# Centring the first two row tiles before their transposes, and applying 1/std when V leaves PSUM

## The chip, the cores and the metric

The kernel runs on one core of a Trainium2 chip. A core has a matrix engine (TensorE, PE in the profile), a vector engine (VectorE, DVE), an activation engine (ScalarE, ACT), a general engine (GpSimd, POOL) and a queue engine that issues most DMAs (SyncE, SP). Each of them works through its own instructions in order and waits on semaphores for the others. The metric is the device time of one execution in microseconds; less is better.

## The reference

One transformer layer on 2048 rows of 1024 in bf16: pre-norm attention with 32 heads of width 32 and a causal window of 256, then a feed-forward part of width 3584, each with a residual. The norm has no weights.

```python
def _layernorm(x, axis=-1, eps=1e-5):
    m = jnp.mean(x, axis=axis, keepdims=True)
    v = jnp.var(x, axis=axis, keepdims=True)
    return (x - m) / jnp.sqrt(v + eps)

x = A_x
h = x + _A_ref(_layernorm(x, axis=-1), A_wqkv, A_wo)
h2 = h + _B_ref(_layernorm(h, axis=-1), B_w1, B_w2)
```

Here `_A_ref` computes `qkv = x @ wqkv`, the windowed softmax attention and the product with `wo`; `_B_ref` is `silu(x @ w1) @ w2`. What matters for the change is that `(x - m) / std` times a weight matrix is the same as `(x - m)` times that matrix with each row divided by its std afterwards.

## The kernel before

The 2048 rows are four blocks of 512, each of four row tiles of 128. For a block, the rows are normalised (`ln_stats`, `ln_root`, `ln_norm`), transposed into `lnT_b` (features on the partitions), and multiplied with the weights: `v_group(b, j, c)` makes 512 columns of V for one row tile, `qk_group` makes 128 columns of Q or K for a whole block. Each group is eight matmuls of 128x512 into one PSUM bank (`next_acc` goes round the banks in `acc_banks`), and one copy takes the bank to SBUF. Later blocks, the attention and the feed-forward part are woven together so that TensorE always has matmuls.

The order on each engine is the order in which the Python code calls it; a manual schedule is set, so nothing is reordered. DMAs go out in order on the queue that issues them, SP for nearly all.

The change lies in the head, which makes block 0's V while the first rows and weights still arrive. Its steps before:

- SP issues row tile 0, the first half of the V weights (columns 0 to 511 of V, 1 MB, `load_wqkv(2 * D)`), row tile 2, the second half, row tile 3 and the first 512 Q columns. ACT's queue issues row tile 1 (L135, L139).
- A memset on VectorE (L157) feeds eleven matmuls on zeros (L162), which keep TensorE busy until there is data.
- For row tile 0: statistics on VectorE (L166, L174), the square root on ACT (L201), the reciprocal on VectorE (L208), and the normalisation in four quarters, three on VectorE (L194) and one on ACT (L217). Each quarter is turned by two TensorE transposes (L223), and ACT copies the result from PSUM to `lnT_b` (L224, `turn_first`).
- Row tile 1 the same with all quarters on VectorE. Row tile 2 is normalised in one instruction and turned by TensorE later. Row tile 3 is normalised in one instruction and turned by one DMA transpose that SP issues (L198, `ln_transpose`).
- Behind that transpose SP issues the remaining three loads of Q and K weights (L139), then the four row tiles of block 1 (L135).
- TensorE's order: transposes of tile 0; V of tile 0, columns 0 to 511, with the transposes of tile 1 among its matmuls and those of the next group; V of tile 1, columns 0 to 511; V of tiles 0 and 1, columns 512 to 1023, with tile 2's transposes between; V of tiles 2 and 3; then Q and K (L245, L255). ACT copies V out of PSUM (L247), two banks in turn.
- While Q and K of block 0 run, their banks are emptied by ACT and VectorE in turn (L257), and VectorE does the statistics of block 1 between its own copies.

Of the kernel before, what the change touches and what calls it, by code (L numbers as in the profile page):

```python
# [9 lines left out]
F32 = mybir.dt.float32  # L10
I32 = mybir.dt.int32
ACT = mybir.ActivationFunctionType
ALU = mybir.AluOpType

P = 128
# [29 lines left out]
def kernel(  # L45
# [10 lines left out]
    nc = tc.nc  # L56
# [3 lines left out]
    S, D = x2d.shape  # L60
# [4 lines left out]
    KT = D // P  # L65
# [4 lines left out]
    scale = float(DH) ** -0.5  # L70

    const = ctx.enter_context(tc.tile_pool(name="const", bufs=1))
    small = ctx.enter_context(tc.tile_pool(name="small", bufs=2))
# [12 lines left out]
    r_e = big.tile([P, 13312], BF16, name="r_e")  # L86
# [4 lines left out]
    tp_ps = [tp_pool.tile([P, 1024], BF16, name=f"tp{i}") for i in range(4)]  # L91
    o_ps = [ps.tile([P, 8, 64], F32, name=f"o_ps{i}") for i in range(2)]
    acc_ps = [ps.tile([P, 512], F32, name=f"acc{i}") for i in range(2)]

    def view(region, off, *dims):
        n = 1
        for d in dims:
            n *= d
        ap = region[:, off:off + n]
        if len(dims) == 2:  # L100
            return ap.rearrange("p (a b) -> p a b", b=dims[1])
        if len(dims) == 3:
            return ap.rearrange("p (a b c) -> p a b c", b=dims[1], c=dims[2])
        return ap
# [4 lines left out]
    lnT_b = [view(r_w, 24576, KT, 512), view(r_t, 0, KT, 512)]  # L109
    x_ring = [view(r_o, i * 1024, 1024) for i in range(8)]  # L110
# [17 lines left out]
    wqkv_v = A_wqkv.rearrange("(kt p) n -> p kt n", p=P)  # L128
# [5 lines left out]
    def load_x(b, j, queue=nc.sync):  # L134
        queue.dma_start(out=x_ring[(b % 2) * 4 + j], in_=x2d[(b * 4 + j) * P:(b * 4 + j + 1) * P, :])  # L135

    def load_wqkv(c0):
        dst = wqk[:, :, c0:c0 + 512] if c0 < 2 * D else wv[:, :, c0 - 2 * D:c0 - 2 * D + 512]
        nc.sync.dma_start(out=dst, in_=wqkv_v[:, :, c0:c0 + 512])  # L139

    eps = const.tile([P, 1], F32, name="eps")
    nc.vector.memset(eps[:], LN_EPS)
# [1 line left out]
    nc.scalar.activation(out=dummy[:], in_=eps[:], func=ACT.Sqrt)  # L144

    load_x(0, 0)
    load_wqkv(2 * D)
    load_x(0, 1, nc.scalar)
    load_x(0, 2)
    load_wqkv(2 * D + 512)  # L150
    load_x(0, 3)
    load_wqkv(0)

    ident = const.tile([P, P], BF16, name="ident")
    make_identity(nc, ident[:])
    warm = view(r_e, 0, 2, 512)
    nc.vector.memset(warm, 0.0)  # L157
    nc.gpsimd.memset(v[:, :, :, DH:VW], 1.0)


    for i in range(11):
        nc.tensor.matmul(o_ps[i % 2][:].rearrange("p a b -> p (a b)"), lhsT=warm[:, 0, 0:P], rhs=warm[:, 0, :], start=True, stop=True)  # L162


    def ln_half(xt, stats, c):
        nc.vector.bn_stats(out=stats[:, c, :], in_=xt[:, c * 512:(c + 1) * 512])  # L166

    def ln_stats(xt, st, j, half_done=None):
        stats = half_done
        if stats is None:  # L170
            stats = small.tile([P, 2, 6], F32, name="ln_st", tag="ln_st")
            ln_half(xt, stats, 0)
        ln_half(xt, stats, 1)
        nc.vector.bn_aggr(out=st[:, j, :], in_=stats[:])  # L174
# [18 lines left out]
    def ln_norm(xt, st, rs, j):  # L193
        nc.vector.tensor_scalar(out=xt, in0=xt, scalar1=st[:, j, 0:1], scalar2=rs[:, j:j + 1],  # L194
                                op0=ALU.subtract, op1=ALU.mult)

    def ln_transpose(xt, dst, j):
        nc.sync.dma_start_transpose(out=dst[:, :, j * P:(j + 1) * P], in_=xt)  # L198

    def ln_root(st, rs, j):  # L200
        nc.scalar.activation(out=rs[:, j:j + 1], in_=st[:, j, 1:2], func=ACT.Sqrt, bias=eps[:], scale=1.0)  # L201

    def ln_first(xt, st, rs, j, parts, on_act=0):

        if on_act:
            shift = small.tile([P, 2], F32, name="ln_shift", tag="ln_shift")
            nc.scalar.activation(out=shift[:, 0:1], in_=st[:, j, 0:1], func=ACT.Identity, scale=-1.0)
        nc.vector.reciprocal(out=rs[:, j:j + 1], in_=rs[:, j:j + 1])  # L208
        if on_act:
            nc.scalar.activation(out=shift[:, 1:2], in_=shift[:, 0:1], func=ACT.Identity, scale=rs[:, j:j + 1])  # L210
        n = 1024 // parts
        for h in range(parts):
            part = xt[:, h * n:(h + 1) * n]
            if h < parts - on_act:
                ln_norm(part, st, rs, j)
            else:
                nc.scalar.activation(out=part, in_=part, func=ACT.Identity, bias=shift[:, 1:2], scale=rs[:, j:j + 1])  # L217

    def turn_first(j, h):

        for i in range(2):
            kt = h * 2 + i
            nc.tensor.transpose(out=tp_ps[h][:, i * P:(i + 1) * P], in_=x_ring[j][:, kt * P:(kt + 1) * P], identity=ident[:])  # L223
        nc.scalar.copy(out=lnT_b[0][:, h * 2:(h + 1) * 2, j * P:(j + 1) * P],  # L224
                       in_=tp_ps[h][:, 0:256].rearrange("p (k q) -> p k q", q=P))

# [7 lines left out]
    acc_banks = list(a[:] for a in acc_ps)  # L234
# [5 lines left out]
    def v_group(b, j, c, copy, between=None):  # L240
        acc = next_acc()
        for kt in range(KT):
            if between:
                between(kt)
            nc.tensor.matmul(acc, lhsT=lnT_b[b % 2][:, kt, j * P:(j + 1) * P], rhs=wv[:, kt, c * 512:(c + 1) * 512],  # L245
                             start=(kt == 0), stop=(kt == KT - 1))
        copy(out=v[:, b * 4 + j, c * 16:(c + 1) * 16, 0:DH], in_=acc.rearrange("p (h d) -> p h d", d=DH))  # L247
# [204 lines left out]
    dve, act = nc.vector.tensor_copy, nc.scalar.copy  # L452


    st, rs = ln_tiles("a")
    half = small.tile([P, 2, 6], F32, name="ln_st", tag="ln_st")
    ln_stats(x_ring[0], st, 0)
    ln_root(st, rs, 0)
    ln_half(x_ring[1], half, 0)
    ln_first(x_ring[0], st, rs, 0, 4, 1)  # L460
    ln_stats(x_ring[1], st, 1, half)
    for h in range(4):
        turn_first(0, h)
        if h == 2:
            ln_root(st, rs, 1)
    ln_first(x_ring[1], st, rs, 1, 4)
    ln_stats(x_ring[2], st, 2)

    held = []

    def turn_1(kt):
        if kt == 7:
            turn_first(1, 0)

    def turn_1_rest(kt):
        if kt == 2:
            turn_first(1, 3)
            act(**held.pop())
            ln_root(st, rs, 2)

    v_group(0, 0, 0, lambda **args: held.append(args), turn_1)
    turn_first(1, 1)
    turn_first(1, 2)
    v_group(0, 1, 0, act, turn_1_rest)
    ln_first(x_ring[2], st, rs, 2, 1)
    ln_stats(x_ring[3], st, 3)
    ln_root(st, rs, 3)
    ln_first(x_ring[3], st, rs, 3, 1)
    ln_transpose(x_ring[3], lnT_b[0], 3)
    for c0 in (D, 512, D + 512):  # L490
        load_wqkv(c0)
    v_group(0, 0, 1, act)
    for h in range(4):
        turn_first(2, h)
    v_group(0, 1, 1, act)
    v_group(0, 2, 0, act)
    v_group(0, 2, 1, act)
    nc.scalar.activation(out=dummy[:], in_=eps[:], func=ACT.Exp)
    v_group(0, 3, 0, act)
    v_group(0, 3, 1, act)  # L500

    ps_tp.__exit__(None, None, None)
    ps_sc = tc.tile_pool(name="ps_sc", bufs=1, space=bass.MemoryType.PSUM, reuse_waits="tile")
# [214 lines left out]
```

The softmax here doesn't subtract the row's maximum and nothing guards it: scores larger than these inputs give would overflow.

## Time and profile before

| | |
|---|---|
| median of 9 runs | 692.93 us (692.89 to 693.18) |
| the profiled execution | 692.96 us |
| its span, first to last instruction | 691.0 us |
| TensorE busy | 676.7 us, 98% of the span |
| VectorE, ACT, POOL busy | 290.6, 241.9, 161.0 us |
| first matmul on data (V) | 7.51 us after the span's start |
| first matmul of Q and K | 22.41 us |
| granted TensorE clock | 1.00 throughout |

Times in the profile are counted from the span's start. A row of the timeline gives start, duration, engine, line, operation, the tile written and the tiles read, the shapes, a count where like instructions were merged, and in brackets how long the engine was idle before and what released it. `SPq` and `ACTq` are instructions that issue DMAs; their duration is that of the issue, and the time until the data is there is given for a line as "DMA to landing".

### The profile page before, as it was taken

How to read it: one execution, taken by the hardware profiler on the slowest of the kernel's cores; microseconds unless marked ns; L12 is line 12 of the kernel's file. 1: busy time of each engine (PE TensorE's matmuls, PEld its weight loads, DVE VectorE, ACT ScalarE, POOL GpSimd, SP SyncE). 2: the span in 40 equal slices, each digit the busy share in tenths (PEclk: the TensorE clock that was granted, in tenths of full speed). 3: DMA queues.
4: the chain of work that ended last, by engine and by line, in shares of the span. 5: the costliest groups of instructions: out<-in, count | busy, mean ns of one | idle time of the engine just before them, and what ended most of it. 6: DMA issues, size and time to landing. Idle time of an engine off the chain costs nothing.

```text
span 691.0 us, 14107 instructions
## 1 busy us (share of the span) xinstructions
PE 676.7 (98%) x5895; PEld 331.6 (48%) x6011; DVE 290.6 (42%) x609; ACT 241.9 (35%) x463; POOL 161.0 (23%) x295
## 2 busy tenths in 40 slices
PE   8999999999999999999999999999999999999998
PEld 3444555555555555544444444444444444444445
DVE  5267646744444449533316133343133251333111
ACT  5326666666676666421310033300133100233000
POOL 1007666666666656500000000000000000000000
PEclk9999999999999999999999999999999999999999
DMA  7732241136241989971023410022300024100010
GB/s 255 246 59 74 40 89 51 26 63 184 72 131 17 243 235 288 212 270 52 11 83 110 91 39 0 1 91 69 85 0 1 25 88 94 39 1 1 30 39 24
DMA packets 76463, 60.95 MB, mean 88 GB/s; under 512 B 50288, under 2 KB 60528, under 8 KB 76400
## 3 DMA queue, kind: packets, MB, share of 16 engines
q1 hardware_dynamic: 76256, 59.78, 31.7%
q8 instruction: 47, 0.77, 0.4%
q10 hardware_dynamic: 144, 0.26, 0.1%
q14 instruction: 16, 0.13, 0.1%
HBM read 39.85 MB, written 8.39 MB: 70 GB/s over the span
## 4 chain that ended last, share of the span: by engine, by line
PE 97%; issue 1%; DMA 1%; SPq 0%; DVE 0%
PE hacc L628 19%; PE hacc L665 17%; PE acc L255 16%; PE acc L665 10%; PE acc L628 9%; PE acc L245 8%; PE acc L276 7%; PE o_ps L388 5%; PE sc L308 3%; PE hacc L276 1%; DMA r_w<-in_A_wqkv_dram 1%; PE sc L360 1%; PE sc L334 1%; PE tp L223 0%; SPq L135 0%
## 5 line engine op out<-in xcount | busy, mean ns | idle before, releaser
L378 POOL TENSOR_SCALAR_AFFINE_SELECT r_e<-r_e 128x512 bf16<-128x512 bf16 (+1 forms) x288 | 158.0, 564 | 125.6 <-ACT r_e L368 62.1
L665 PEld LDWEIGHTS <-r_a 128*128 128x128 bf16 x952 | 90.9, 98 | 103.0
L628 PEld LDWEIGHTS <-r_w 128*128 128x128 bf16 x896 | 87.4, 98 | 105.0
L665 PE MATMUL hacc<-r_a 128*128 128x512 bf16 (+2 forms) x607 | 121.8, 359 | 0.5
L628 PE MATMUL hacc<-r_e,r_w 128*128 128x512 bf16 x444 | 99.7, 379 | 0.5
L320 ACT ACTIVATE r_e<-sc 128x768 bf16<-128x768 f32 x96 | 78.2, 814 | 48.3 <-PE sc L308 48.3
L637 ACT ACTIVATE r_n<-hacc 128x512 f32<-128x512 f32 x30 | 17.9, 597 | 178.9 <-PE hacc L628 175.5
L665 PE MATMUL acc<-r_a 128*128 128x512 bf16 x329 | 73.5, 379 | 0.4
L255 PEld LDWEIGHTS <-r_w 128*128 128x128 bf16 x512 | 44.2, 97 | 46.2 <-issue 1.0
L255 PE MATMUL acc<-r_t,r_w 128*128 128x512 bf16 x233 | 60.3, 379 | 2.4 <-issue 1.7
L257 DVE CAST r_a<-acc 128x512 bf16<-128x512 f32 x56 | 38.6, 690 | 56.5 <-PE acc L255 43.6
L255 PE MATMUL acc<-r_w 128*128 128x512 bf16 x240 | 58.0, 379 | 1.5 <-issue 1.0
L388 PEld LDWEIGHTS <-r_e 128*128 128x128 bf16 x1440 | 47.4, 96 | 17.9
L276 PE MATMUL acc<-r_o,r_a 128*128 128x512 bf16 x188 | 49.5, 379 | 1.9 <-issue 1.3
L628 PE MATMUL acc<-r_e,r_w 128*128 128x512 bf16 x213 | 48.9, 379 | 0.3
L388 PE MATMUL o_ps<-r_a,r_e 128*128 128x33 bf16 x1440 | 48.1, 178 | 0.1
L680 DVE SCALAR_TENSOR_TENSOR r_t<-hacc,r_t 128x512 bf16<-128x512 f32 (+2 forms) x22 | 14.0, 635 | 56.6 <-PE hacc L665 55.2
L321 ACT ACTIVATE r_e<-sc 128x256 bf16<-128x256 f32 x96 | 37.4, 390 | 0.0
L680 DVE SCALAR_TENSOR_TENSOR r_t<-acc,r_t 128x512 bf16<-128x512 f32 x12 | 8.3, 692 | 64.2 <-PE acc L665 58.8
L638 DVE SCALAR_TENSOR_TENSOR r_a<-r_n,hacc 128x512 bf16<-128x512 f32 x30 | 20.7, 688 | 33.0 <-ACT r_n L637 33.0
L628 PE MATMUL hacc<-r_a,r_w 128*128 128x512 bf16 x139 | 32.6, 379 | 0.3
L276 PEld LDWEIGHTS <-r_a 128*128 128x128 bf16 x256 | 21.8, 97 | 22.3
(79 smaller groups left out, 532.0 us busy)
## 6 DMA issues: line engine op xcount, KB each, us to landing
r_w<-in_B_w_dram SPq DMA_DIRECT2D x8, 896.0 KB, 5.0
r_a<-in_B_w_dram SPq DMA_DIRECT2D x7, 1024.0 KB, 7.3
r_w<-in_A_wqkv_dram SPq DMA_DIRECT2D x6, 1024.0 KB, 9.0
h_dram<-r_t SPq DMA_DIRECT2D x16, 256.0 KB, 2.7
r_t<-h_dram SPq DMA_DIRECT2D x16, 256.0 KB, 2.9
out_dram<-r_t SPq DMA_DIRECT2D x31, 128.0 KB, 1.7
r_o<-in_A_x_dram SPq DMA_DIRECT2D x15, 256.0 KB, 4.0
r_e<-h_dram SPq DMA_DIRECT2D x3, 1024.0 KB, 5.6
```

The costliest lines, as they stand in the source:

```text
L245: nc.tensor.matmul(acc, lhsT=lnT_b[b % 2][:, kt, j * P:(j + 1) * P], rhs=wv[:, kt, c * 512:(c + 1) * 512], start=(kt == 0), stop=(kt == KT ...
L255: nc.tensor.matmul(acc, lhsT=wqk[:, kt, col0:col0 + P], rhs=lnT_b[b % 2][:, kt, :], start=(kt == 0), stop=(kt == KT - 1))
L257: copy(out=(qT, kT)[which][b][:, g, :], in_=acc)
L276: nc.tensor.matmul(acc, lhsT=qT[b][:, g, j * P:(j + 1) * P], rhs=wo[:, g, c * 512:(c + 1) * 512], start=(g == 0), stop=(g == G - 1))
L308: nc.tensor.matmul(sc[hh // 2][half * 64:half * 64 + 64, hh % 2, col:col + qb - qa], lhsT=kT[t // 4][r0:r0 + DH, g, k0:k0 + 64], rhs=qT[b] ...
L320: nc.scalar.activation(out=tri[:, :, :, 64:256], in_=both, func=ACT.Exp, scale=scale)
L321: nc.scalar.activation(out=e[:, 1024:1280].rearrange("p (h q) -> p h q", q=P), in_=bank[:, :, 192:320], func=ACT.Exp, scale=scale)
L378: nc.gpsimd.affine_select(out=dst, in_=src, pattern=[[0, n] for n in dst.shape[1:-1]] + [[sgn, P]], compare_op=ALU.is_ge if upper else ALU ...
L388: nc.tensor.matmul(o_ps[pair][:, qt * 2 + hh, 0:VW], lhsT=chunk_of(i, bank, piece, pair, hh), rhs=v[:, b * 4 + kt, g * 4 + pair * 2 + hh, ...
L628: nc.tensor.matmul(acc, lhsT=w1[:, kt, ft * P:(ft + 1) * P], rhs=ln2T[b][:, kt, :], start=(kt == 0), stop=(kt == KT - 1))
L665: nc.tensor.matmul(acc[:, 0:c1 - c0], lhsT=gT[:, ft, j * P:(j + 1) * P], rhs=w2[ft // 4][:, ft % 4, c0:c1], start=(ft == 0), stop=(ft == F ...
L680: nc.vector.scalar_tensor_tensor(out=t_out[j % 2][:, c0:c1], in0=acc[:, 0:c1 - c0], scalar=0.5, in1=t_in[j % 2][:, c0:c1], op0=ALU.mult, o ...
```

## The change

Row tiles 0 and 1 are no longer normalised before they are turned. Their means are found first (for tile 0 half by ACT with a summed activation and half by VectorE's statistics, for tile 1 by ACT alone), VectorE writes centred copies into `x_mid` in quarters, and these are turned and used for V. The four V groups of tiles 0 and 1 are held in four PSUM banks (the two of `o_ps` are added for the time), and ACT empties them with 1/std as the scale of each row. The statistics, roots and reciprocals are placed by when these evacuations and tile 2 need them; tile 2's copies from PSUM come ahead of the last held evacuation. Q and K need fully normalised rows, so tiles 0 and 1 are also normalised in place later, and turned by two more DMA transposes, issued behind tile 3's and ahead of the three weight loads.

Around it: row tile 1 is loaded on SP's queue, second; the halves of the V weights come in four and two pieces; the warm-up's memset covers 128 columns and its matmuls, nine in place of eleven, read them with a repeated pattern.

```diff
-    def load_wqkv(c0):
+    def load_wqkv(c0, parts=1):
         dst = wqk[:, :, c0:c0 + 512] if c0 < 2 * D else wv[:, :, c0 - 2 * D:c0 - 2 * D + 512]
-        nc.sync.dma_start(out=dst, in_=wqkv_v[:, :, c0:c0 + 512])
+        n = KT // parts
+        for k in range(0, KT, n):
+            nc.sync.dma_start(out=dst[:, k:k + n, :], in_=wqkv_v[:, k:k + n, c0:c0 + 512])
+
+    warm = view(r_e, 0, P)
+    nc.vector.memset(warm, 0.0)
...
     load_x(0, 0)
-    load_wqkv(2 * D)
-    load_x(0, 1, nc.scalar)
+    load_x(0, 1)
+    load_wqkv(2 * D, 4)
     load_x(0, 2)
-    load_wqkv(2 * D + 512)
+    load_wqkv(2 * D + 512, 2)
     load_x(0, 3)
     load_wqkv(0)
...
-    for i in range(11):
-        nc.tensor.matmul(o_ps[i % 2][:].rearrange("p a b -> p (a b)"), lhsT=warm[:, 0, 0:P], rhs=warm[:, 0, :], start=True, stop=True)
+    wide = bass.AP(tensor=warm.tensor, offset=warm.offset, ap=[warm.ap[0], [0, 4], warm.ap[1]])
+    for i in range(9):
+        nc.tensor.matmul(o_ps[i % 2][:].rearrange("p (a c) b -> p a (c b)", c=2), lhsT=warm, rhs=wide, start=True, stop=True)
...
+    x_mid = [view(r_e, 1024 + 1024 * j, 1024) for j in range(2)]
+    scrap = view(r_e, 3072, 1024)
+    mean = small.tile([P, 3], F32, name="mean")
+    half = small.tile([P, 2, 6], F32, name="ln_half")
+
+    def mean_first():
+
+        nc.scalar.activation(out=scrap[:, 0:512], in_=x_ring[0][:, 512:1024], func=ACT.Identity, scale=-1.0 / D, accum_out=mean[:, 0:1])
+        ln_half(x_ring[0], half, 0)
+        nc.vector.tensor_scalar(out=mean[:, 1:2], in0=half[:, 0, 1:2], scalar1=half[:, 0, 4:5], scalar2=-0.25, op0=ALU.add, op1=ALU.mult)
+        nc.scalar.activation(out=scrap, in_=x_ring[1], func=ACT.Identity, scale=-1.0 / D, accum_out=mean[:, 2:3])
+
+    def center(j):
+        for h in range(4):
+            out, in0 = (x[j][:, h * 256:(h + 1) * 256] for x in (x_mid, x_ring))
+            if j == 0:
+                nc.vector.tensor_scalar(out=out, in0=in0, scalar1=mean[:, 0:1], scalar2=mean[:, 1:2], op0=ALU.add, op1=ALU.add)
+            else:
+                nc.vector.tensor_scalar(out=out, in0=in0, scalar1=mean[:, 2:3], scalar2=None, op0=ALU.add)
+
+    held = []
+
+    def hold(**args):
+        held.append(args)
+
+    def scaled(j):
+        args = held.pop(0)
+        nc.scalar.activation(func=ACT.Identity, scale=rs[:, j:j + 1], **args)
+
+    def place(at):
+        return lambda kt: turn_first(*at[kt], x_mid[at[kt][0]]) if kt in at else None
+
+    acc_banks += [o[:].rearrange("p a b -> p (a b)") for o in o_ps]
+    mean_first()
+    center(0)
+    center(1)
+    turn_first(0, 0, x_mid[0])
+    turn_first(0, 1, x_mid[0])
+    v_group(0, 0, 0, hold, place({1: (0, 2), 3: (0, 3), 5: (1, 0), 6: (1, 1), 7: (1, 2)}))
+    turn_first(1, 3, x_mid[1])
+    ln_stats(x_ring[2], st, 2)
+    ln_root(st, rs, 2)
+    ln_stats(x_ring[0], st, 0, half)
     ln_root(st, rs, 0)
+    ln_recip(rs, 2)
+    ln_norm(x_ring[2], st, rs, 2)
+    ln_recip(rs, 0)
+    ln_stats(x_ring[1], st, 1)
+    ln_root(st, rs, 1)
+    v_group(0, 1, 0, hold)
+    v_group(0, 0, 1, hold)
+    scaled(0)
+    ln_recip(rs, 1)
+    scaled(1)
+    scaled(0)
+    ln_stats(x_ring[3], st, 3)
+    v_group(0, 1, 1, hold)
     for h in range(4):
+        turn_first(2, h, x_ring[2])
+        if h == 1:
+            ln_root(st, rs, 3)
+    scaled(1)
+    ln_norm(x_ring[0], st, rs, 0)
+    ln_recip(rs, 3)
+    ln_norm(x_ring[3], st, rs, 3)
+    ln_norm(x_ring[1], st, rs, 1)
+    for j in (3, 0, 1):
+        ln_transpose(x_ring[j], lnT_b[0], j)
     for c0 in (D, 512, D + 512):
         load_wqkv(c0)
-    v_group(0, 0, 1, act)
-    for h in range(4):
-        turn_first(2, h)
-    v_group(0, 1, 1, act)
     v_group(0, 2, 0, act)
     v_group(0, 2, 1, act)
     nc.scalar.activation(out=dummy[:], in_=eps[:], func=ACT.Exp)
     v_group(0, 3, 0, act)
     v_group(0, 3, 1, act)
+    del acc_banks[2:]
```

## The prediction

> **What bounds the kernel now.** I read the page first: who is busy and who stands on the chain.
>
> ```profile
> PE 676.7 (98%) x5895; PEld 331.6 (48%) x6011; DVE 290.6 (42%) x609; ACT 241.9 (35%) x463; POOL 161.0 (23%) x295
> ...
> PE 97%; issue 1%; DMA 1%; SPq 0%; DVE 0%
> ```
>
> TensorE is the bound, so time can only be won or lost where it waits, and a shift of it early in the run reaches the end. The change touches only the first 22 us, so next comes the chain in order of time for the first 60 us.
>
> ```profile
> 1.26 6.21 DMA r_w<-in_A_wqkv_dram
> ...
> 7.51 1.67 PE acc L245 x7
> ...
> 13.95 8.63 PE acc L245 x40
> ```
>
> TensorE's first useful matmul starts at 7.51, when the first half of the V weights has landed (7.47). Seven take 1.67, which is 0.216 us from start to start. From there to 22.41, where Q and K begin, it hardly waits. Up to 1.5 us can be won ahead of 7.51; anything that arrives late afterwards is lost in full. So I then read, in the timeline, what arrives when.
>
> ```profile
> 5.23 0.21 DVE L174 BATCH_NORM_AGGREGATE st_a<-ln_st 128x2 f32<-128x12 f32 x1
> 5.36 0.64 DVE L166 BATCH_NORM_STATS2 ln_st<-r_o 128x6 f32<-128x512 bf16 x1
> ...
> 9.39 1.28 DVE L166 BATCH_NORM_STATS2 ln_st<-r_o 128x6 f32<-128x512 bf16 x2
> ...
> 10.71 0.21 DVE L174 BATCH_NORM_AGGREGATE st_a<-ln_st 128x2 f32<-128x12 f32 x1
> 10.78 0.59 ACT L478 CAST r_a<-acc 128x512 bf16<-128x512 f32 x1
> ...
> 11.26 0.31 ACT L201 ACTIVATE rs_a<-st_a,eps 128x1 f32<-128x1 f32 x1
> ...
> 11.80 0.55 DVE L194 TENSOR_SCALAR r_o<-r_o,st_a,rs_a 128x1024 bf16<-128x1024 bf16 x1
> ...
> 12.26 1.28 DVE L166 BATCH_NORM_STATS2 ln_st<-r_o 128x6 f32<-128x512 bf16 x2
> ...
> 14.92 1.33 SPq L198 DMA_TRANSPOSE r_w<-r_o  x1
> ...
> 16.29 2.59 SPq L139 DMA_DIRECT2D r_w<-in_A_wqkv_dram  x3
> ...
> 18.93 5.15 SPq L135 DMA_DIRECT2D r_o<-in_A_x_dram  x4
> ...
> 30.13 1.28 DVE L166 BATCH_NORM_STATS2 ln_st<-r_o 128x6 f32<-128x512 bf16 x2
> ...
> 32.98 0.69 DVE L257 CAST r_a<-acc 128x512 bf16<-128x512 f32 x1 [1.33 <-PE acc L255]
> ```
>
> Three readings: VectorE spends 1.45 us on one tile's statistics (9.39 to 10.71, then 0.13 until the next instruction can start, as 5.23 to 5.36 shows). Tile 3's DMA transpose, T3, is issued at 14.92, and SP starts the next three weight loads only behind it. Block 1's statistics start at 30.13, right behind a copy, so their rows were there. The instructions of one line, looked at one DMA at a time, give the landings: tile 2's load, T3, and the first row tile of block 1.
>
> ```profile
> L135 SPq DMA_DIRECT2D r_o<-in_A_x_dram x1: 582/582/582, 1.7 to 1.7; - x1
> DMA to landing us min/median/max: 6.4/6.4/6.4
> ```
>
> ```profile
> L198 SPq DMA_TRANSPOSE r_w<-r_o x1: 1326/1326/1326, 14.9 to 14.9; - x1
> DMA to landing us min/median/max: 3.2/3.2/3.2
> ```
>
> ```profile
> L135 SPq DMA_DIRECT2D r_o<-in_A_x_dram x1: 3087/3087/3087, 18.9 to 18.9; - x1
> DMA to landing us min/median/max: 10.8/10.8/10.8
> ```
>
> So tile 2 is there at 1.73 + 6.42 = 8.15, T3 at 18.14 and block 1's first tile at 29.72.
>
> **The head, part by part.** The sum is against the profiled execution, 692.96 us (span 691.0 and 1.96 around it); the median of nine is 692.93, 0.03 less.
>
> Warm-up: the memset falls from 0.48 us to 0.06 or so (an eighth of the elements), so TensorE starts near 1.1 in place of 1.55, and 9 matmuls at 0.43 end near 4.95. Nothing waits for them. POOL's queue keeps its order (identity, then the ones beside V, busy until 3.63 as before), and the one load taken off ACT's queue stood beside its table load, so neither moves anything.
>
> Loads: tile 1 moves from the ACT queue to the second place on SP's, and the V weights come in 4 and 2 pieces. That is 4 more issues of 0.4 to 0.6 us on SP, hidden because the DMA engines are saturated: 344 GB/s from 2.0 to 7.25. The bytes ahead of tile 2 are the same (x0, x1, half the V weights), so I leave its landing at 8.15. Bounds: 7.3 (1.84 MB have moved by 7.25) and 8.45. The first piece, behind 0.79 MB, lands near 5.2; the fourth near 7.4, where the whole landed before.
>
> Centring: tile 0 lands at 3.9. Half its statistics (0.61) stand beside ACT's sum of the other half (a 128x512 ACTIVATE, 0.6), plus one small VectorE step of 0.18: mean at 4.75, first quarter centred at 5.1 (0.35; 0.26 from start to start). ACT must then sum tile 1 (128x1024: 1.02) before its first copy, so until 5.65; the copy takes 0.37. First V matmul at about 6.05, 1.46 earlier. The price of reading out ACT's sum is in no row: from nothing to 0.3 (one more 128x1 ACTIVATE, L201); I take 0.1. The group then runs at the pace of weight pieces and copies and ends near 8.45, against 9.35. Three more groups, 24 x 0.216 = 5.2, end near 13.75, and eight transposes of tile 2 at 14.2. The four groups sit in four PSUM banks, so none waits for its evacuation.
>
> VectorE's centring (8 x 0.26) ends near 6.8 to 7.2, ahead of tile 2's rows. So VectorE waits for 8.15 whatever the head has won.
>
> **The path of T3.** From 8.15: tile 2's statistics 1.45 (9.60); second half and aggregate of tile 0, 0.71 + 0.13 (10.44); reciprocal 0.18, norm of tile 2 0.46 (11.80 to 12.26), reciprocal 0.15 (11.23); tile 1's statistics with their aggregate 1.53 (12.76). Now ACT: root 1, 0.04 + 0.20 (13.00). Behind it in ACT's order stand three held evacuations, now with a scale per row: no row has this form. From below, a CAST of the same tile holds ACT 0.48 (10.78 to 11.26); from above, add the 0.23 by which the 128x256 ACTIVATE with two pointer operands (L217, 0.60) exceeds a 128x256 COPY (0.37): 0.71. One pointer is halfway, 0.60: 1.80 (14.80). Two copies of tile 2 at 0.26 (15.32), root 3 0.32 (15.64), reciprocal 0.18, norm of tile 3 0.55: T3 is issued at 16.4, 1.5 later than before. VectorE itself is ready for that reciprocal at 15.2 (1.45 for tile 3 from 13.3, 0.46 for tile 0), so ACT's queue sets it.
>
> T3 lands 3.2 later, at 19.6. Pairs of such transposes issued back to back near 387 us also took 3.2. TensorE would come for it at 18.7 (ACT's first copy of tile 2 ends at 15.17, then 16 x 0.216) and waits until 19.7. Before, that matmul ran at 22.41 - 3.45 = 18.96. **Shift: +0.7.** T0 and T1, two added issues of 1.33, land by 22.3, ahead of Q and K at 23.15: covered by 0.8.
>
> SP's queue: the weight loads and block 1's rows are issued behind three transposes, at 16.4 + 4.0 = 20.4 in place of 16.29, so 4.1 later. The weights have 7 us of slack (the first landed at 21.9 for use at 29.3). Block 1's first rows land at 33.9; their statistics (1.45) stand in VectorE's order ahead of a K group's evacuation (0.69), which ends near 36.0. Two groups later TensorE needs that PSUM bank, at 34.7 + 0.7 = 35.4. **Another +0.65.** Bounds: 0, if the rows' lag on the slowest DMA engine (first engine done at 27.84, last at 29.71) does not recur; 0.9.
>
> Sum: +1.35, so 694.3 against the median. The whole of it is T3's issue time less 15.05, and no gain of the head enters.
>
> The rule that speaks against the change: in this trace the weight loads of the warm-up stand 0.43 apart up to 5.37, and useful matmuls 0.216 apart from 7.51; the fast clock came some 3.9 us after the start. The Trainium skill (TensorE: Matmul & The Clock Gate, "What's actually happening") says that TensorE runs at half clock until about one 3.4 us window was busy, and that windows run free. By it, warm-up work of 3.85 us barely fills one, and with an unlucky phase the first group would run cold; the sum would be that of the second rival below, while by the row's 3.9 us the clock is there at 5.0 and the sum stays.
>
> **The rivals.** (1) Tile 2 lands early, as alone on the queue. At 6.85, when VectorE is free, everything behind moves 1.3 earlier: T3 at 15.1, landed at 18.3, and the sum is about +0.05: 693.0, not slower. For it: x0 alone took only 3.1 us. Against it: the bytes. It decides from a landing 1.3 earlier than summed. (2) TensorE stays at half clock after the warm-up: the first group's 8 matmuls and 10 transposes cost 8 x 0.43 + 10 x 0.11 = 4.5 from 6.05, ending at 10.6 instead of 8.45. Tile 2's copies and root 3 then come 0.7 to 1.8 later: +2.0 to +3.1, say 695.4. Against it: the same warm-up time sufficed before. (3) Block 1's rows are not late: only +0.7, 693.6. (4) The centring wins nothing at 7.51: still 694.3, since VectorE waits for tile 2.
>
> **How the numbers follow.** The measurement tells 0.2%, 1.39 us, from no change. Main case 0.62: T3's issue between 15.9 and 17.0 by the prices above, so 693.8 to 694.9, a little under half of it beyond 694.3. Rival 1: 0.15; rival 2: 0.15; rival 3: 0.08. Rival 4 changes nothing. Slower by over 0.2%: 0.29 + 0.15 = 0.44. Faster needs the whole head's 1.4 with nothing late: 0.04. Rest: 0.52. The range leaves one in ten at either end: 692.6 (tile 2 early and evacuations at 0.48) to 695.5 (rival 2's middle).
>
> **What would show it.** Right: first L236 matmul near 6.1; VectorE idle before tile 2's BATCH_NORM_STATS2 near 8.1; T3 issued near 16.4; TensorE idle about 1 us before the first V matmul of tile 3; a VectorE wait on block 1's rows near 32 and a second TensorE gap near 35. Wrong: T3 issued by 15.1, tile 2's statistics starting near 7, or matmuls 0.43 apart after 6.

## The result, and the profile after

The changed kernel takes 694.93 us (median of 10 runs, 693.92 to 697.43). The kernel before, run beside it on the same chip, takes 692.99 us (30 runs, 692.77 to 693.48). The change makes it slower, by 1.94 us in the medians. The ratio of the recorded comparison, which is not that of the medians, is 1.0034 with a 95% interval of 1.0026 to 1.0042, or 2.4 us: three of the ten runs lie above 696. One execution of the kernel before, in the job of g1_best, ran at a granted clock of 0.75 (878.63 us) and enters no comparison below. The profiled execution of the changed kernel took 694.60 us (span 692.9), 1.64 us more than the profiled execution of before and 0.33 below its own median.

The page of the changed kernel, busy times first and then the shares of the chain that ended last:

```profile
PE 677.0 (98%) x5893; PEld 331.6 (48%) x6009; DVE 291.4 (42%) x613; ACT 243.4 (35%) x464; POOL 160.9 (23%) x295
...
PE 93%; DMA 2%; issue 2%; SPq 1%; DVE 1%; ACT 0%
```

TensorE has the same work (677.0 us against 676.7), but only 93% of the chain is now TensorE's, against 97%. The chain itself, in order of time for the first 45 us (start, duration, what):

```profile
3.73 4.97 DMA r_o<-in_A_x_dram
8.72 1.30 DVE ln_st L170 x2
...
13.96 1.26 ACT r_a L474 x2
15.22 0.54 ACT r_w L215 x2
15.76 0.20 ACT rs_a L205
...
16.19 1.01 DVE r_o L198 x2
17.20 0.89 SPq L202
18.20 1.27 SPq L202
19.65 1.24 SPq L202
20.94 0.57 SPq L141
...
23.57 10.80 DMA r_o<-in_A_x_dram
34.40 1.30 DVE ln_st L170 x2
...
36.54 10.09 PE acc L246 x46
```

Up to 36.54 no TensorE piece stands in these rows. The chain is tile 2's landing (8.70), VectorE's statistics, two held evacuations on ACT, two copies of tile 2, root 3, its reciprocal and norm, then SP with three transposes and three weight loads, and at last block 1's rows.

The timeline of the changed kernel shows the two places where TensorE pays. The first is T3, tile 3's DMA transpose:

```profile
5.75 0.61 PE L236 MATMUL acc<-r_w 128*128 128x512 bf16 x1 [0.25 <-ACT r_w L215]
...
8.72 1.29 DVE L170 BATCH_NORM_STATS2 ln_st<-r_o 128x6 f32<-128x512 bf16 x2 [2.43 <-DMA r_o<-in_A_x_dram]
...
13.39 0.67 ACT L474 ACTIVATE r_a<-acc,rs_a 128x512 bf16<-128x512 f32 x1
...
15.62 0.33 ACT L205 ACTIVATE rs_a<-st_a,eps 128x1 f32<-128x1 f32 x1
...
15.99 0.16 DVE L208 RECIPROCAL rs_a<-rs_a 128x1 f32<-128x1 f32 x1 [0.46 <-ACT rs_a L205]
...
16.76 4.13 SPq L202 DMA_TRANSPOSE r_w<-r_o  x3
...
20.10 1.25 PE L236 MATMUL o_ps<-r_w 128*128 128x512 bf16 x5 [0.93 <-DMA r_w<-r_o]
```

Useful matmuls begin 1.76 us earlier than before (5.75 against 7.51). VectorE then stands idle for 2.43 us until tile 2 is there. T3 is issued at 16.76, 1.84 later than before, and TensorE waits for it. Q and K begin at 23.56, against 22.41.

A row's idle time counts from the modelled end of a matmul (0.38 us long), though the next can follow 0.216 after its start. Below, a gap is what stands from start to start beyond that pace, 0.16 more than the row's idle time: 1.09 here for 0.93, and 0.89 for the 0.73 at the second place.

The second place is block 1's rows, whose landing the instructions of the load's line give, taken one DMA at a time:

```profile
L135 SPq DMA_DIRECT2D r_o<-in_A_x_dram x1: 3226/3226/3226, 23.6 to 23.6; - x1
DMA to landing us min/median/max: 10.8/10.8/10.8
```

```profile
30.67 0.69 DVE L248 CAST r_a<-acc 128x512 bf16<-128x512 f32 x1 [2.69 <-PE acc L246]
34.40 1.29 DVE L170 BATCH_NORM_STATS2 ln_st<-r_o 128x6 f32<-128x512 bf16 x2 [3.04 <-DMA r_o<-in_A_x_dram]
35.85 0.64 DVE L248 CAST r_a<-acc 128x512 bf16<-128x512 f32 x1
36.54 4.69 PE L246 MATMUL acc<-r_w 128*128 128x512 bf16 x21 [0.73 <-DVE r_a L248]
```

The rows land at 34.4 (29.7 before). VectorE has been standing in front of their statistics since 31.4, with the next PSUM copy behind them in its order, so the copy comes late and TensorE waits for the bank.

One landmark tells how much of a run is decided here: the first piece of the chain that reads `PE sc`, a score matmul. It stands at 50.20 before and at 52.24 after. From there to the end of the span it is 640.6 to 640.9 us in all 14 profiled executions of this study. Whatever these kernels differ in lies ahead of it. The shift of 2.04 us at the landmark is 1.15 at the first Q and K matmul and 0.89 at the second gap. The time grew by less, 1.64, since the parts behind the landmark and outside the span came out 0.4 us shorter in that execution.

### The profile page after: what moved, and what is told of

Its sections match the earlier page's. It is cut to its first block, busy times and chain, and to the rows that moved or that the text cites. A ratio compares the mean times of both kernels' runs of the same rounds, so it can differ in the third digit from the quotient of the medians.

```text
span 692.9 us, 14118 instructions
## 1 busy us (share of the span) xinstructions
PE 677.0 (98%) x5893; PEld 331.6 (48%) x6009; DVE 291.4 (42%) x613; ACT 243.4 (35%) x464; POOL 160.9 (23%) x295
## 4 chain that ended last, share of the span: by engine, by line
PE 93%; DMA 2%; issue 2%; SPq 1%; DVE 1%; ACT 0%
PE hacc L650 18%; PE hacc L687 17%; PE acc L246 14%; PE acc L687 10%; PE acc L650 9%; PE acc L267 7%; PE acc L236 6%; PE o_ps L379 5%; PE sc L299 3%; DMA r_o<-in_A_x_dram 2%; PE hacc L267 1%; PE sc L351 1%; SPq L141 1%; PE sc L325 1%; DVE ln_st L170 1%
```

## The experiments

My theory is the forecast's: T3 late (first gap), and block 1's rows queued behind three transposes (second gap). The rivals are the half clock in the first group, the loads in pieces as the cause of late landings, and the head's gain being lost on TensorE itself. All experiment kernels compute the whole reference. Medians of before in the four jobs were 693.24, 693.21, 693.21 and 693.16, but 692.99 beside the changed kernel, so a gain over the changed kernel's 694.93 that is read from medians alone comes out some 0.2 us too small. The ratios, each against before in its own job, are free of that. Their intervals reach 0.6 us to either side and more where runs are few, so a gain under about 0.8 us over the changed kernel is not told from none by the times.

| kernel | median us (lowest to highest, runs) | ratio to before, 95% interval | landmark in its profile |
|---|---|---|---|
| changed kernel | 694.93 (693.92 to 697.43, 10) | 1.0034 [1.0026, 1.0042] | 52.24 |
| e1_x_early | 694.14 (693.82 to 695.47, 11) | 1.0015 [1.0006, 1.0024] | 52.31 |
| e2_stats_order | 694.89 (694.40 to 696.58, 5) | 1.0032 [1.0019, 1.0045] | 54.17 |
| e3_t3_freed | 693.77 (693.21 to 695.95, 11) | 1.0013 [1.0004, 1.0022] | 51.16 |
| e4_both | 693.01 (692.11 to 694.10, 11) | 0.9996 [0.9987, 1.0005] | 51.68 |
| e5_both_unsplit | 697.53 (697.34 to 698.24, 5) | 1.0062 [1.0049, 1.0074] | 54.77 |
| e6_before_pieces | 693.16 (692.54 to 693.64, 11) | 0.9998 [0.9989, 1.0007] | 49.88 |
| e7_before_again | 693.47 (1 run) | none | 50.80 |
| e8_warm11 | 694.99 (694.77 to 696.89, 6) | 1.0029 [1.0017, 1.0040] | 52.55 |
| f1_t2_early | 693.26 (692.26 to 693.84, 11) | 0.9997 [0.9988, 1.0006] | 51.08 |
| f2_t0_first | 692.88 (692.47 to 693.45, 11) | 0.9994 [0.9985, 1.0003] | 50.01 |
| f3_root3_only | 694.63 (694.03 to 696.41, 11) | 1.0020 [1.0011, 1.0029] | 53.75 |
| g1_best | 692.32 (692.04 to 693.06, 11) | 0.9989 [0.9979, 0.9998] | 49.87 |

Several profiled executions lie high within their kernel's own range (those of e2, f3 and e4 at or near its upper end). So what an edit is worth is read from the medians, and what happens from the profiles.

### Block 1's rows ahead of two weight loads

The changed kernel, with one thing moved on SP's queue:

```diff
-    for c0 in (D, 512, D + 512):
+    load_wqkv(D)
+    for j in range(4):
+        load_x(1, j)
+    for c0 in (512, D + 512):
         load_wqkv(c0)
...
-    for j in range(4):
-        load_x(1, j)
```

> One thing moved: SP issues block 1's four row loads behind the first of the three late weight loads, ahead of the other two. Theory (late rows): TensorE's second gap, 0.88 us near 35.5 in the changed kernel's profile, goes; the first gap before tile 3's V (1.1) stays. So about 0.9 less than the changed kernel: 694.0 against 694.9. Rival (clock): the loss lies in the first V group, which ran partly at half clock; then nothing changes, 694.9. If the rows were late for another reason than their place in the queue, also 694.9.

694.14 us, 0.79 less than the changed kernel (1.3 by the ratios). In its timeline VectorE no longer waits for the rows:

```profile
31.63 0.69 DVE L248 CAST r_a<-acc 128x512 bf16<-128x512 f32 x1 [2.69 <-PE acc L246]
32.23 1.28 DVE L170 BATCH_NORM_STATS2 ln_st<-r_o 128x6 f32<-128x512 bf16 x2
```

The statistics follow the copy directly, as they did before the change, and the second gap is gone. The first gap stays (1.12 us in this profile). So the second gap is what the forecast said it was, worth 0.8 us by the medians. This profiled execution also shows what the first gap hangs on: tile 2 landed at 9.63, 0.93 later than in the profile of the changed kernel, and T3 was issued at 17.68, 0.92 later. From tile 2's landing to T3's issue it is 8.06 us in the changed kernel, 8.05 here and 8.05 in e8_warm11 below: with this order of work T3 follows tile 2's rows one to one.

### Statistics of tiles 0 and 1 ahead of tile 2's

The changed kernel, with VectorE's 2.43 us of idle time filled:

```diff
-    ln_stats(x_ring[2], st, 2)
-    ln_root(st, rs, 2)
     ln_stats(x_ring[0], st, 0, half)
     ln_root(st, rs, 0)
-    ln_recip(rs, 2)
-    ln_norm(x_ring[2], st, rs, 2)
-    ln_recip(rs, 0)
     ln_stats(x_ring[1], st, 1)
     ln_root(st, rs, 1)
+    ln_stats(x_ring[2], st, 2)
+    ln_root(st, rs, 2)
+    ln_recip(rs, 0)
+    ln_recip(rs, 2)
+    ln_norm(x_ring[2], st, rs, 2)
```

> One thing moved: the statistics and roots of tiles 0 and 1 come ahead of tile 2's on VectorE and ACT, into the 2.4 us in which VectorE waited for tile 2's rows. Theory (ACT's queue holds root 3 behind three held evacuations and two copies): T3's issue moves only from 16.8 to about 16.1, so 0.7 less than the changed kernel, 694.2. Rival (VectorE's chain alone sets T3): all 2.3 us are won there, T3 near 14.5, and the time falls by 1.5 or more, to 693.4 or less. Rival (clock): no change.

694.89 us: no gain, a miss. The timeline of that kernel says why:

```profile
9.12 1.29 DVE L170 BATCH_NORM_STATS2 ln_st<-r_o 128x6 f32<-128x512 bf16 x2 [0.49 <-DMA r_o<-in_A_x_dram]
...
13.02 1.29 DVE L170 BATCH_NORM_STATS2 ln_st<-r_o 128x6 f32<-128x512 bf16 x2 [1.19 <-DMA r_o<-in_A_x_dram]
...
14.90 0.61 PE L214 MATMUL tp<-ident,r_o 128*128 128x128 bf16 x8
15.21 0.65 ACT L215 COPY r_w<-tp 128x256 bf16<-128x256 bf16 x2 [1.15 <-PE tp L214]
```

VectorE reached tile 3's statistics 1.19 us before tile 3's rows were there, started at once when they landed, and was done by 14.6. So with this order tile 3's own landing (12.99) comes into T3's path, a bound that the forecast and the expectation had left out. Root 3 came later still: it stands on ACT behind two copies of tile 2, and these wait for tile 2's transposes on TensorE, which stand behind the third and fourth V group and ran at 14.90. In this profile VectorE waited 1.13 us for root 3, so ACT's place for it held T3 (16.86), and not VectorE's time. From tile 2's landing to T3 it is 7.76 us, 0.30 less than in the changed kernel.

### Root 3 ahead of tile 2's copies

The kernel of the last experiment, with root 3 moved on ACT and the norms of tiles 0 and 1 moved ahead of tile 3's statistics on VectorE:

```diff
     scaled(0)
+    ln_norm(x_ring[0], st, rs, 0)
+    ln_norm(x_ring[1], st, rs, 1)
     ln_stats(x_ring[3], st, 3)
+    ln_root(st, rs, 3)
+    ln_recip(rs, 3)
+    ln_norm(x_ring[3], st, rs, 3)
     v_group(0, 1, 1, hold)
     for h in range(4):
         turn_first(2, h, x_ring[2])
-        if h == 1:
-            ln_root(st, rs, 3)
     scaled(1)
-    ln_norm(x_ring[0], st, rs, 0)
-    ln_recip(rs, 3)
-    ln_norm(x_ring[3], st, rs, 3)
-    ln_norm(x_ring[1], st, rs, 1)
```

> As the run before, and root 3 ahead of tile 2's copies on ACT, with tiles 0 and 1 normalised ahead of tile 3's statistics. Theory: T3 is issued near 14.9 as in the kernel before, TensorE's gap before tile 3's V goes, and the rows of block 1 land 1.8 earlier, so that most of the second gap goes too: 692.6 to 693.1, with runs closer together. Rival (clock): 694.9 as the changed kernel, since the head is the same.

693.77 us, 1.16 less than the changed kernel (1.5 by the ratios), but above the expected 693.1 at most: a miss in size. Its timeline:

```profile
12.97 1.29 DVE L170 BATCH_NORM_STATS2 ln_st<-r_o 128x6 f32<-128x512 bf16 x2
...
14.54 0.29 ACT L205 ACTIVATE rs_a<-st_a,eps 128x1 f32<-128x1 f32 x1 [0.49 <-DVE st_a L178]
15.20 1.20 ACT L215 COPY r_w<-tp 128x256 bf16<-128x256 bf16 x4 [0.36 <-PE tp L214]
15.64 4.08 SPq L202 DMA_TRANSPOSE r_w<-r_o  x3
...
17.36 2.97 PE L236 MATMUL o_ps<-r_w 128*128 128x512 bf16 x13
```

T3 goes out at 15.64, tile 3's matmuls run on behind tile 2's, and Q and K begin at 22.54. The second gap is still there (0.84 us). So the first gap is T3, worth 1.2 us by the medians.

T3 was expected near 14.9, and the second gap to go for the most part. Neither came, and the first row tells why: tile 3's statistics start when tile 3's rows land (12.95), and T3 follows 2.69 us later. It is 2.69 in e4_both and g1_best below too. With both orders mended it is tile 3's landing that sets T3, where in the changed kernel its rows had been there since 12.37 and were read at 13.60.

### Both edits

The kernel of the last experiment, with block 1's rows moved as in the first.

> The run before and the early row loads of the first run together. Theory: neither gap is left; what stays is TensorE's wait for tile 2's copies (0.8 in the changed kernel) against the 1.5 us by which V starts earlier: 692.3 to 692.7, faster than the kernel before by 0.3 to 0.7. Rival (clock): 694.9. Rival (something else in the head is late, such as the weight pieces): 693.0 or more.

693.01 us, 1.92 less than the changed kernel; the two edits alone give 0.79 + 1.16 = 1.95. By the ratios it is 2.6, against 1.3 and 1.5. So the two gaps add up as far as the noise allows, and they make up the whole loss: with both gone the time is that of before (0.9996, interval 0.9987 to 1.0005). The expected gain over before did not come: the median lies at the lower edge of what the last rival named, something else in the head that is late.

### Root 3 alone

The changed kernel again, to price ACT's order without the order of the statistics:

```diff
     ln_stats(x_ring[3], st, 3)
+    ln_root(st, rs, 3)
     v_group(0, 1, 1, hold)
     for h in range(4):
         turn_first(2, h, x_ring[2])
-        if h == 1:
-            ln_root(st, rs, 3)
     scaled(1)
-    ln_norm(x_ring[0], st, rs, 0)
     ln_recip(rs, 3)
     ln_norm(x_ring[3], st, rs, 3)
+    ln_norm(x_ring[0], st, rs, 0)
     ln_norm(x_ring[1], st, rs, 1)
```

> The changed kernel with one thing moved: root 3 (and with it the norm of tile 3 ahead of tile 0's) ahead of tile 2's copies on ACT. The statistics stay in their order. Theory (ACT's queue held root 3 by about half a us, the statistics' order by the rest): T3 is issued 0.4 to 0.5 earlier, 694.4 to 694.6 against 694.9. If the statistics' order alone were the cause, no change; if root 3's place alone were, 693.8 as with both moved.

694.63 us, 0.30 less by the medians (1.0 by the ratios). Alone, ACT's order gives 0.30 and VectorE's order 0.04, and the times tell neither from nothing; together they give 1.16. The profiles are clearer: from tile 2's landing to T3 it is 8.06 us in the changed kernel, 7.76 with VectorE's order mended, 7.54 with ACT's, and 6.37 with both. With one of them mended, the other still holds T3.

In the profile of this kernel tile 2 landed at 10.55, the latest of all, and T3 went out at 18.10, with root 3 in the better place. Something else is seen there: TensorE waited for a piece of the V weights, and then ran at half clock up to 11.2 (the second row is that of a window from 8 to 11 us, its columns as explained below).

```profile
8.08 0.59 PE L236 MATMUL acc<-r_w 128*128 128x512 bf16 x1 [1.35 <-DMA r_w<-in_A_wqkv_dram]
```

```profile
8.00:11.00 3.00, 2.92 (x13) 1.46 (x13) 0.42 (x1) 1.09 (x3) 0.00 (x0) 0.50 1.02 353
```

### The loads: pieces, and the kernel before once more

Three runs ask whether the added pieces make the landings late. First, the kernel with both edits and the V weights in one piece for each half:

```diff
     load_x(0, 1)
-    load_wqkv(2 * D, 4)
+    load_wqkv(2 * D)
     load_x(0, 2)
-    load_wqkv(2 * D + 512, 2)
+    load_wqkv(2 * D + 512)
     load_x(0, 3)
```

> The version with both gaps removed, but the V weights in one piece per half as in the kernel before. Question: why do tile 2's and tile 3's rows land late and at times that change from run to run (8.7 to 10.0 for tile 2 in five profiles, 8.1 before). Theory (pieces): the pieces make the stream of the head slower; without them tile 2 lands near 8.1, few packets in the head are longer than 0.18 us (3 before, 21 to 41 with pieces), the runs lie within 0.8 us of each other, and the first V matmul goes back to 7.5; time 693.2 to 693.7. Rival (chance, or row tile 1's new place): tile 2 still lands at 8.7 or later and the runs spread over 2 us.

697.53 us, 4.5 more than with pieces: a miss. Tile 2 landed at 10.01, no earlier. The timeline of TensorE, and the table of windows between 7.25 and 12 us (window, its length, then busy time and count of PE, PEld, DVE, ACT and POOL, the granted clock, the DMA share, GB/s):

```profile
5.24 0.54 PE L214 MATMUL tp<-ident,r_e 128*128 128x128 bf16 x4 [0.61 <-DVE r_e L463]
9.36 0.58 PE L236 MATMUL acc<-r_w 128*128 128x512 bf16 x1 [3.59 <-DMA r_w<-in_A_wqkv_dram]
9.96 1.06 PE L236 MATMUL acc<-r_w 128*128 128x512 bf16 x2
```

```profile
7.25:7.50 0.25, 0.00 (x0) 0.00 (x0) 0.21 (x3) 0.00 (x0) 0.00 (x0) 0.90 1.00 303
7.50:7.75 0.25, 0.00 (x0) 0.00 (x0) 0.25 (x2) 0.00 (x0) 0.00 (x0) 0.50 0.98 332
```

```profile
8.00:12.00 4.00, 2.64 (x11) 1.24 (x11) 2.43 (x6) 0.74 (x2) 0.00 (x0) 0.50 1.07 364
```

The first half of the V weights landed whole at 9.32. TensorE had nothing to do from 5.6 to 9.36, and then ran at a granted clock of 0.50, its matmuls 0.43 us apart until 14.0. At full clock the work of these 4.6 us would have taken about half as long, so some 2.3 us of the loss, as an estimate, is the clock; the rest goes with the late start. The Trainium skill (TensorE: Matmul & The Clock Gate, "HAM oscillation") gives the rule that TensorE is not to idle for more than about 3.4 us, or it runs cold again. The rows here are stricter: the gap is 3.75 us long, but the granted clock fell near 7.45, not 2 us into it, and in the profile of f3_root3_only it fell in a gap of 1.5 us, 1.35 by its row (0.89 on the mean of 7 to 8 us, 0.50 behind it). So the pieces keep TensorE busy early, and with it the clock.

Second, the kernel before with the changed loads (tile 1 second on SP's queue, V weights in 4 and 2 pieces):

```diff
     load_x(0, 0)
-    load_wqkv(2 * D)
-    load_x(0, 1, nc.scalar)
+    load_x(0, 1)
+    load_wqkv(2 * D, 4)
     load_x(0, 2)
-    load_wqkv(2 * D + 512)
+    load_wqkv(2 * D + 512, 2)
     load_x(0, 3)
```

> The kernel before with only the loads changed: row tile 1 second on SP's queue, V weights in four and two pieces. Theory (pieces): tile 2 lands at 8.7 or later and differently from run to run, and the runs spread over 1 to 2 us; VectorE reaches tile 2 only at 9.4 there, so the median rises by little, 0 to 0.8. Rival (the spread comes from the centred design): as the kernel before, 692.9 to 693.2, runs within 0.6.

693.16 us, ratio 0.9998: the loads by themselves change nothing, and the times spread no more than those of before. Tile 2 landed at 8.77 here, as late as in the changed kernel, and the kernel before did not mind: Q and K began at 22.09.

Third, one more look at the kernel before, unchanged.

> The kernel before, unchanged, for a second look at its head. Theory (pieces): tile 2 lands between 8.0 and 8.4 again, and under 10 packets of the head are longer than 0.18 us. Rival (chance): a landing at 8.7 or later, or 20 and more long packets.

693.47 us, a single run. Its landing of tile 2, by the load's line:

```profile
L135 SPq DMA_DIRECT2D r_o<-in_A_x_dram x1: 572/572/572, 1.7 to 1.7; - x1
DMA to landing us min/median/max: 7.0/7.0/7.0
```

7.0 us in place of the 6.4 on which the forecast was built, for the same instruction of the same kernel. From 2 to 5 us its DMA engines moved 267 GB/s, against 330 in the first profile, as the last column of the window shows:

```profile
2.00:5.00 3.00, 3.00 (x9) 1.08 (x8) 0.58 (x1) 0.28 (x2) 1.63 (x1) 1.00 0.96 267
```

In the packet records up to 15.5 us, 29 packets took over 0.18 us, and only 3 in the first profile of before; eight other profiles counted have 21 to 43. Over the profiled executions tile 2 landed between 8.14 and 10.55, and the first profile of before holds the earliest. So landings scatter, with and without the change. The rival that blames the pieces falls: without them tile 2 landed at 10.01 in e5_both_unsplit, and long packets are in e7_before_again too. Whether the new order of the loads (tile 1 second on SP's queue) makes tile 2 later on the whole is not shown: without it there are two profiles (8.14 and 8.74), with it twelve (8.59 to 10.55), and no run moved tile 1 back in the changed kernel. Why packets are long in some executions stays open.

### Two more warm-up matmuls

The changed kernel, against the rival of the half clock:

```diff
-    for i in range(9):
+    for i in range(11):
```

> The changed kernel with eleven warm-up matmuls in place of nine. Theory (T3 and late rows): no change in time, 694.9, although the first V group begins up to 0.8 later and runs at full clock; TensorE only waits less for tile 2's copies and tile 3's transpose. Rival (clock): the first group at half clock cost up to 1 us, so the time falls to 694.2 or less.

694.99 us, the same as the changed kernel within its spread. TensorE in its timeline:

```profile
6.60 0.39 PE L236 MATMUL acc<-r_w 128*128 128x512 bf16 x1 [0.25 <-ACT r_w L215]
...
6.94 0.59 PE L236 MATMUL acc<-r_w 128*128 128x512 bf16 x2
```

In the changed kernel the first two V matmuls take 0.40 and 0.43 us, the third is still slow at its start (6.79), and only from 7.17 they stand 0.216 apart. Here the first starts 0.85 us later and all run at 0.216. (The page's granted clock reads 1.00 in both, and even in the warm-up, where matmuls stand 0.43 apart; the half speed at the start is read from the spacing.) The spread of the times alone could hide a us, but the trace shows that nothing hangs on the head: T3 follows tile 2's landing by 8.05 us as before, and the gaps for T3 and for block 1's rows are 1.08 and 1.01 us. So the half speed is real for those matmuls and costs nothing, and 0.85 us of head start is worth nothing either, as the forecast had it.

### Tile 2's transposes earlier, and tile 0's DMA transpose first

With both gaps gone the kernel is level with before, so the head's gain must be lost elsewhere. Three more steps, each on the one before it, starting from the kernel with both edits. First, tile 2's transposes ahead of the fourth V group:

```diff
     ln_stats(x_ring[3], st, 3)
+    for h in range(4):
+        turn_first(2, h, x_ring[2])
     ln_root(st, rs, 3)
...
     v_group(0, 1, 1, hold)
-    for h in range(4):
-        turn_first(2, h, x_ring[2])
     scaled(1)
```

> The version with both gaps removed, and tile 2's transposes ahead of the fourth V group, so that their copies run beside it. Theory: TensorE's wait for tile 2's copies (0.77 in the changed kernel, 0.3 with both gaps removed) goes too; what is left are waits for the second half of the V weights. 692.3 to 693.0, against 693.0 for both. If the weights' arrival bounds this stretch in any case, no change: 693.0.

693.26 us against 693.01: no gain (693.0 to 693.3 is level within the spread). Root 3 stands behind four copies again, T3 went out at 16.47, and TensorE waited 0.69 us for it. Then, tile 0's DMA transpose ahead of T3, which VectorE could have ready earlier:

```diff
-    for j in (3, 0, 1):
+    for j in (0, 3, 1):
         ln_transpose(x_ring[j], lnT_b[0], j)
```

> The run before, with tile 0's added DMA transpose issued ahead of tile 3's. Tile 0 is free for it as soon as its V groups are done. Theory: the last of the three lands up to 1.4 earlier, so that Q and K do not wait for it (0.64 in one profile of the version with both gaps removed): 0 to 0.5 less than the run before. If tile 0's transpose pushes tile 3's behind 15.5 + 3.2, TensorE waits there instead and the run is slower by up to 1.

692.88 us. SP's queue starts at 12.78, T3 follows at 15.52, and root 3 is still awaited:

```profile
12.78 5.36 SPq L202 DMA_TRANSPOSE r_w<-r_o  x3
...
14.74 0.16 DVE L208 RECIPROCAL rs_a<-rs_a 128x1 f32<-128x1 f32 x1 [0.78 <-ACT rs_a L205]
...
18.76 1.04 PE L236 MATMUL o_ps<-r_w 128*128 128x512 bf16 x4 [0.42 <-DMA r_w<-r_o]
```

Last, root 3 behind the second copy in place of the fourth:

```diff
         turn_first(2, h, x_ring[2])
-    ln_root(st, rs, 3)
+        if h == 1:
+            ln_root(st, rs, 3)
     ln_recip(rs, 3)
```

> The run with tile 0's transpose first, and root 3 behind the second of tile 2's four copies on ACT in place of the fourth. Theory: T3 was issued at 15.5 there, with VectorE waiting 0.8 for root 3 and TensorE 0.6 for T3's data; root 3 can run 0.5 earlier, so T3 is issued near 15.0 and TensorE's wait shrinks to 0.1: 692.3 to 692.6, against 692.9 for the run before and 693.2 for the kernel before. If the weights' and rows' arrival bounds this stretch, no change: 692.9.

692.32 us, ratio 0.9989 [0.9979, 0.9998]: 2.61 us less than the changed kernel and 0.8 less than the kernel before in the same job. Its timeline:

```profile
13.09 4.90 SPq L202 DMA_TRANSPOSE r_w<-r_o  x3
...
14.60 0.16 DVE L208 RECIPROCAL rs_a<-rs_a 128x1 f32<-128x1 f32 x1 [0.36 <-ACT rs_a L205]
...
16.75 3.54 PE L236 MATMUL o_ps<-r_w 128*128 128x512 bf16 x15
```

Tile 3's matmuls run without a wait, and Q and K begin at 22.07. That is only 0.34 us earlier than in the profile of before, though the first V matmul ran 1.5 us earlier (6.00). What is left on its chain is the second half of the V weights:

```profile
4.72 7.24 DMA r_w<-in_A_wqkv_dram
...
11.99 1.02 PE o_ps L236 x4
```

TensorE is idle for 0.46 us before the last piece of that half, and goes on at 11.99 with its 21st V matmul. In the profile of before the 21st ran at 12.47 (the 24th, the last ahead of tile 2's transposes, stands at 13.12 in its chain, and three take 0.65). So at that point the head start of 1.5 us is worth no more than 0.5. That the weights' landing is what caps this design is read from these rows; no run moved that load to test it.

## Why the prediction was right or wrong

The forecast was 694.3 us, in a range that holds the measured 694.93. It put 0.52 on a time within 0.2% of before and 0.44 on a slower one; the less likely of the two came, with the mechanism of the main case. By its steps:

- **"No gain of the head enters": right.** e8_warm11 delays the head by 0.85 us, and T3 still follows tile 2's landing by the same 8.05 us. The first V matmul came at 5.75 (6.05).
- **Tile 2's landing, 8.15: the term that was mis-sized.** It came at 8.70 in the profile of the changed kernel, beyond the upper bound of 8.45, and anywhere from 8.59 to 10.55 in the others built on it. The one profile of before that it was drawn from has the earliest landing of all. In the kernel before, 0.6 of this cost nothing (e6_before_pieces); here T3 follows it one to one (8.70 and 16.76, 9.63 and 17.68). It would also explain why the changed kernel's times spread by 3.5 us, where those of before beside it spread by 0.7; its slowest runs (697.12 and 697.43) have no profile, so that is not shown.
- **The path from there to T3: right in kind, 0.19 too long.** 8.70 to 16.76 is 8.06; the forecast had 8.25. The scaled evacuation, unseen before, took 0.67 us and 0.57 from start to start (taken: 0.60). ACT did set T3: VectorE waited 0.46 for root 3. Reading out ACT's sum is an instruction of its own of 0.18 us (taken: 0.1).
- **T3's landing: right.** 3.3 after its issue (3.2). With T3 0.36 late, the first shift became 1.15 in place of 0.7.
- **Block 1's rows: right.** Landed at 34.38 (33.9), with a second shift of 0.89 in place of 0.65, inside its bounds. Its worth by removal is 0.79.
- **The rule that the shift is T3's issue less 15.05: nearly right.** It gives 1.71; the profiled execution shows 1.64 in the time and 2.04 at the landmark. In e3_t3_freed, with T3 at 15.64, it gives 0.59, and the profiled execution (693.49) shows 0.53. It needs block 1's rows to stand behind T3 on SP's queue, which e1_x_early ends, and everything between to run as usual: in the profile of e2_stats_order T3 at 16.86 gives 1.81, but the execution shows 3.62, since tile 1's transpose and block 1's rows landed late there.
- **Rival 1 (tile 2 early): wrong,** the landing went the other way. **Rival 2 (half clock): wrong as a cause.** In the changed kernel two to three matmuls ran at half speed, hidden under VectorE's wait, and all its runs read a mean clock of 1.000. But the half clock does occur with this head: in the profile of f3_root3_only it held for 3.4 us, and single runs of e2, e3 and f3 at 695.2 to 696.4 read mean clocks of 0.997 and 0.998 (the kernel before has one such run too, 694.96 at 0.998). **Rival 3 (rows not late): wrong** for the changed kernel; e1_x_early, which makes them early, shows its price. **Rival 4 (no earlier V) did not come:** V began 1.76 us earlier.
- **Left out of the sum:** TensorE's waits for the pieces of the V weights (0.43 at 11.1 in the changed kernel) and for tile 2's copies beyond what was summed (0.77 at 14.71). Both stand ahead of T3's wait and were swallowed by it. Tile 3's own landing (12.37 there) was left out too. Once T3's path was mended, it and the weights became what is left.

The error of size came from trusting one execution's landing as if it were a constant, or as if the new order of the loads could not move it, and so did the balance between "same" and "slower". With tile 2 at 8.70 the same sum would have come to 1.35 + 0.55 = 1.90, beyond the 1.39 that the measurement tells. That this is so close to the 1.94 of the medians is in part luck: the path behind the landing was 0.19 too long, and the execution in which tile 2 landed at 8.70 was slower by 1.64.

## What to carry to other kernels

A load that lands behind megabytes of other loads has no fixed time: before summing a path from its landing, look at several executions, and price the step that now waits for it at its late end. When work is moved ahead of a short instruction that releases a DMA (here root 3 on ACT), follow the whole queue behind that DMA, too; here it held three weight loads and the next block's rows, and TensorE waited at two places, some 0.8 and 1.2 us. And when two engines' orders both hold a step, mending one gives little (the path to T3 grew shorter by 0.30 and 0.52 us here, and by 1.69 with both), so a null result for one edit does not clear its engine. When the times spread by more than the effect, compare such a path between two landmarks of the same profile.

## What the runs showed of the hardware

- Landings at the kernel's start scatter: the same load of the same kernel took 6.4 and 7.0 us in two executions, and tile 2 landed between 8.14 and 10.55 over the profiled executions, with 3 to 43 packets over 0.18 us up to 15.5 us in the ten profiles counted.
- In a gap of 3.75 us without a matmul the granted clock fell to 0.50 near 7.45, and the matmuls stayed 0.43 us apart for 4.6 us after they had resumed (e5_both_unsplit). In f3_root3_only it fell in a gap of 1.5 us (1.35 by its row), and came back near 11.2. When full speed first came differs between executions with the same warm-up of nine matmuls: the matmuls stand 0.216 apart from 3.98 in e3_t3_freed, and only from 7.17 in the changed kernel. So a comparison of nine with eleven from one profile each does not tell what a warm-up needs.
- A 16 KB instruction fetch under way beside a DMA transpose may hold up its landing. In the profile of e2_stats_order the fetch came at 21.6 and tile 1's transpose landed at 24.27, and in that of e4_both it came at 21.1 and the transpose landed at 23.76, 4.5 and 4.6 us after their issue in place of 3.1 to 3.5. TensorE then waited 0.75 and 0.64 us before Q and K. This was seen beside each other in two profiles and was not tested by itself.
